# Attention probabilities of a gated attention + FFN block: one pass over the logits, with the turn done by DMA transposition

## The chip, the core and the metric

The kernel runs on one core of one Trainium2 chip, in one launch. The metric is the device time in microseconds; the time before is 1783.49 us, the median of 3 runs (1783.17 to 1783.70). Engines are named as in the profile: PE (TensorE matmul) and PEld (its weight loads), DVE (VectorE), ACT (ScalarE), POOL (GpSimd) and SP (SyncE, whose queue issues every DMA of this kernel; the profile calls its issuing "SPq").

## The reference, cut to what matters

Two branches read the same x (2048 tokens, 576 features) and are mixed by a gate per token. Branch A is attention with 32 heads of 18 features over 4 segments of 512 tokens, causal within a segment, plus a linear memory of the earlier segments; branch B is a SwiGLU FFN with 4608 hidden features.

```python
for s in range(N):                       # 4 segments of L = 512 tokens
    logits = einsum("bhqd,bhkd->bhqk", qs, ks) * scale + mask      # mask: -1e9 above the diagonal
    p = softmax(logits, axis=-1)
    a_dot = einsum("bhqk,bhkd->bhqd", p, vs)
    a_mem = (phi(qs) @ M) / (phi(qs) @ z + 1e-6)
    outs.append(g * a_mem + (1 - g) * a_dot)
    M, z = M + phi(ks).T @ vs, z + phi(ks).sum(...)
a = concat(outs) @ wo
b = (silu(x @ w_gate) * (x @ w_up)) @ w_down
return gate * a + (1 - gate) * b
```

## The kernel before, in words

Everything is computed to about fp32 accuracy out of sums of rounded terms: an fp32 operand is split into a high part (fp32r, bf16 or fp16) and a rest, and several matmuls are summed in PSUM.

**Stages.** First come the projections q, k, v of all segments and the memory branch (up to about 330 us of the span). q and k go to DRAM (`stk`) as three bf16 terms each. Then the FFN runs in two halves of 1024 tokens. A half has 36 positions, one for each tile of 128 hidden features (the loop at L1043). In a position PE makes seven products for gate and up (`seven`, L1035 and L1038). After every third position 16 groups of the down product (`down_groups`, L874) fall due, and they are worked off in the next position. In half 0 the split weights are also written to DRAM (`wc`, L257); half 1 reads them back (L682). A last stage turns the attention output, multiplies it by wo and mixes (L1160 on).

**Attention beside the FFN.** Attention is a generator, `att_gen` (L807). The hand-written function `beat` (L975) advances it by one step, tau, at chosen points of the FFN's program. In half 0 a step is taken only while down groups are due, so 10 steps stand in every third position and none in the other two; in half 1 the other positions take 4 or 5 steps each as well. The order on each engine is thus fixed by the program's text. One unit u is 2 heads of one segment (64 units, 8 matmuls of each kind a unit), and 5 steps work on the 5 PSUM banks of one unit:

- `s_bank` (L699): logits of query tiles i against keys 0..i, with the queries on the partitions. DVE adds the mask and takes the maximum of each row (L713, the masked logits themselves go to a scratch tile), into `mbs`. At the unit's last bank five small DVE instructions split the maxima into three bf16 terms and turn them in 32x32 blocks (L719 to L728).
- `m_store` (L730) writes those terms to DRAM (4 DMAs a unit) and `row_load` (L192) reads them back as 3 additional rows of `qst` (1 DMA). The `kst` tiles hold -1 in these rows.
- `t_bank` (L747), TL = 12 steps later: the same logits once more, now with the keys on the partitions and 111 rows, so that the maximum is subtracted by the matmul itself (L753). ACT takes Exp out of PSUM (L757), POOL zeroes what lies above the diagonal (L765).
- PL = 2 steps later DVE makes the fp16 high term of the probabilities (L843) and POOL the rest (L845).
- `pv_step` (L769): both terms are the stationary operands, v moves (L782, L784): 40 matmuls a unit. DVE sums the terms of v (L789), `o_step` (L795) divides, and the result goes to DRAM at a later step (`sends`, L812, or L849 at the end).

`stack_loads` (L175, issued at L819) brings in q and k of the next unit: 10 DMAs a unit, into one of NST = 4 buffers. `s_bank`, `t_bank` and `pv_step` share PSUM banks 5, 6 and 7 in turn (`ts_tile`).

All DMAs stand in SP's one queue in program order. In the built program each also waits for the DMA eight before it in that queue (8 semaphores in turn), so at most 8 are under way.

Of the kernel before, what the change touches and what calls it, by code (L numbers as in the profile page):

```python
# [12 lines left out]
F32 = mybir.dt.float32  # L13
# [7 lines left out]
P = 128  # L21
# [4 lines left out]
L = 512  # L26
# [11 lines left out]
NST = 4  # L38
TL = 12
PL = 2  # L40
VL = 3
# [22 lines left out]
def gated_mix(ctx, tc, xT, xrest, wf, wfr, wfh, wd, wv, wo, beta, cmask, ident, bmask, out):  # L64
# [11 lines left out]
    mxd = dram.tile([2 * NB, 3, 8, P], BF, name="mxd")  # L76
# [35 lines left out]
    ts_tile = banks(5, 6, 7)  # L112
# [60 lines left out]
    VP, accs, cur, unit, ms, mts, mbs = {}, {}, {}, {}, {}, {}, []  # L173
# [17 lines left out]

    def row_load(u):  # L192
        nc.sync.dma_start(qst[u % NST][KR:KR + 3].rearrange("z j (i n) -> z (j i) n", n=P), mxd[u])
# [76 lines left out]
    with ExitStack() as st:  # L270
# [293 lines left out]
        for s in range(NSEG):  # L564
# [41 lines left out]
            if s == 3:  # L606
# [4 lines left out]
                for i in range(NST):  # L611
                    if i < 2:
                        qst.append(kq.tile([P, 2, L], BF, name=f"qst{i}"))
                    if i < 2:
                        kst.append(kq.tile([P, 2, L], BF, name=f"kst{i}"))
                for i in range(2):
                    mbs.append(kq.tile([P, 8], F32, name=f"mb{i}"))
# [7 lines left out]
            for n in range(8):  # L625
# [10 lines left out]
                else:  # L636
                    if n == 4:
                        wraw_of[1] = [w_load(1, u) for u in range(2)]
                    if n < 2:
                        first_sum(6, n)  # L640
                    elif n < 6:
                        if n < 4:
                            nc.gpsimd.memset(f32(rhs[n - 2][96:]), 0.0)
                        if n == 3:
                            r_fetch(0)
                        if n - 2 < len(kst):
                            nc.gpsimd.memset(kst[n - 2], -1.0)
# [13 lines left out]
    with ExitStack() as st:  # L661
# [24 lines left out]
        kp = pool(ast, "kp", 2, side="right")  # L686
        ap = pool(ast, "ap", 2, side="right")
        for i in range(2, NST):
            kst.append(kp.tile([P, 2, L], BF, name=f"kst{i}", bufs=1))
        for i in range(2, NST):  # L690
            qst.append(kp.tile([P, 2, L], BF, name=f"qst{i}", bufs=1))
        for i in range(2, NST):
            defer(5 + i, lambda i=i: nc.gpsimd.memset(kst[i], -1.0))
        mqs = [kp.tile([P, 32], BF, name=f"mq{i}", bufs=1) for i in range(2)]
        for i in range(2):
            defer(9 + i, lambda i=i: nc.gpsimd.memset(mqs[i], 0.0))
        SPLAN = [[(0, 0, 3)], [(0, 1, 3)], [(384, 0, 0), (0, 0, 2)], [(384, 1, 0), (0, 1, 2)], [(0, 0, 1), (256, 1, 1)]]

        def s_bank(u, n):  # L699
            qs, ks = qst[u % NST], kst[u % NST]  # L700
            m = mbs[u % 2]
            bank = SPLAN[n]
            t = ts_tile()
            for c, pr, i in bank:
                w = P * (i + 1)
                nc.tensor.matmul(t[:, c:c + w], qs[:KR, pr, P * i:P * i + P], ks[:KR, pr, 0:w],  # L706
                                 start=True, stop=True)
                yield
            for c, pr, i in bank:
# [3 lines left out]
                nc.vector.tensor_tensor_reduce(scr[:, :w], t[:, c:c + w], cm[:, L - w:L], 1.0, -3.0e38,  # L713
                                               OP.add, OP.max, m[:, k:k + 1])
            if n == 4:
                mq = mqs[u % 2][:, :24].rearrange("p (z q) -> p z q", q=8)
                mr = kp.tile([P, 8], F32, name="mr")
                c = -SHIFT / SCALE
                nc.vector.tensor_scalar_add(mq[:, 0], m, c)  # L719
                nc.vector.scalar_tensor_tensor(mr, m, c, mq[:, 0], op0=OP.add, op1=OP.subtract)  # L720
                nc.vector.tensor_copy(mq[:, 1], mr)
                nc.vector.tensor_sub(mq[:, 2], mr, mq[:, 1])
                m_tr(u)
            yield

        def m_tr(u):
            mt = mts[u] = kp.tile([P, 32], BF, name="mt", bufs=1)
            nc.vector.transpose(mt, mqs[u % 2])  # L728

        def m_store(u):  # L730
            mt = mts.pop(u)
            d = mxd[u].rearrange("z q n -> (z q) n")
            for b in range(4):
                nc.sync.dma_start(d[:, 32 * b:32 * b + 32], mt[32 * b:32 * b + 24])

        def blk(pr, j, i):
            if j == 0:
                return pr, P * i
            if j == 1:
                return 2 + pr, P * (i - 1)  # L740
            if j == 3:
                return 2 + pr, 384
            return 4, 256 * pr + P * (i - 2)

        TPLAN = [[(0, 0)], [(1, 0)], [(0, 1), (0, 3)], [(1, 3), (1, 1)], [(0, 2), (1, 2)]]

        def t_bank(u, k):  # L747
            qs, ks = qst[u % NST], kst[u % NST]
            t = ts_tile()
            for pr, j in TPLAN[k]:  # L750
                _, c = blk(pr, j, j)
                w = L - P * j
                nc.tensor.matmul(t[:, c:c + w], ks[:KR + 3, pr, P * j:P * j + P], qs[:KR + 3, pr, P * j:L],  # L753
                                 start=True, stop=True)
                yield
            pe = ap.tile([P, L], F32, name="pe", bufs=4)
            nc.scalar.activation(pe, t, AF.Exp, scale=SCALE)  # L757
            if k < 2:
                d = pe[:, 0:P]
                pat = [[1, P]]  # L760
            else:
                st_ = 384 if k < 4 else 256
                d = bass.AP(tensor=pe.tensor, offset=pe.offset, ap=[pe.ap[0], [st_, 2], [1, P]])
                pat = [[0, 2], [1, P]]
            nc.gpsimd.affine_select(d, d, pattern=pat, compare_op=OP.is_ge, fill=0.0, base=0, channel_multiplier=-1)  # L765
            cur[5 * u + k] = pe
            yield

        def pv_step(z):  # L769
            u, k = divmod(z, 5)  # L770
            g, hf = divmod(u, 2)
            s, b = divmod(u, 16)
            if k == 0:
                unit[u] = ts_tile([P, 2, 4, 3 * E])
            t = unit[u]
            p1, p2 = cur.pop(("p", z))
            todo = [(pr, i, j) for pr, j in TPLAN[k] for i in range(j, 4)]
            for n, (pr, i, j) in enumerate(todo):
                h = 2 * b + pr
                v = VP[4 * s + h // 8][:, j, h % 8].rearrange("p t e -> p (t e)")  # L780
                c = blk(pr, j, i)[1]
                nc.tensor.matmul(t[:, pr, i, :], p1[:, c:c + P], v, start=(k == 0 and n == 0), stop=False,  # L782
                                 skip_group_check=True)
                nc.tensor.matmul(t[:, pr, i, 0:2 * E], p2[:, c:c + P], v[:, 0:2 * E], start=False,  # L784
                                 stop=(k == 4 and n == len(todo) - 1), skip_group_check=True)
            if k == 4:
# [20 lines left out]
        def att_gen():  # L807
            N = 10 * NB
            for tau in range(N + TL + VL + 5):
# [10 lines left out]
                z = tau - TL - VL - 1  # L820
# [420 lines left out]
```

## Time and profile before

| | us |
|---|---|
| median of 3 runs | 1783.49 |
| span of the profiled execution (first to last instruction) | 1782.1 |
| PE busy, 12381 matmuls | 1770.7 (99%) |
| PEld busy | 1521.5 (85%) |
| DVE busy | 1281.8 (72%) |
| ACT busy | 939.6 (53%) |
| POOL busy | 831.9 (47%) |
| DMA queue of the kernel, share of 16 engines | 61.0% |

The profiled execution has no time of its own besides its span; the median of the runs lies 1.4 us above it, which is what lies around the span. Busy times are unions of what ran on an engine; matmuls are pipelined, so the mean duration in a row is longer than what a matmul adds to a chain. SP's issuing isn't in the table of busy times; it is seen in the timeline of SP and in the views of single lines. The granted clock of PE is 1.000 over the whole span.

### The profile page before, as it was taken

Reading aid. Unit: us, or ns where it says so; the run is one execution under the profiler, and the core shown is the slowest. Engines: PE = TensorE matmul, PEld = TensorE weight load, DVE = VectorE, ACT = ScalarE, POOL = GpSimd, SP = SyncE. Lnnn points to the kernel's source line nnn. Section 1 sums busy time; section 2 is a strip of 40 time slices with the busy share of each in tenths; the row PEclk is TensorE's granted clock in tenths of the full one; section 3 lists DMA queues with packets and bytes.
Section 4 is the critical chain, followed back from the end, with each engine's and each line's share of the span. In section 5 each row is a group of like instructions: output and inputs, shape, how many; then the busy total and the mean of one; then the engine's idle time right before and its main releaser. Section 6 shows DMA issues by size and latency. Waiting matters only on the chain.

```text
span 1782.1 us, 36452 instructions
## 1 busy us (share of the span) xinstructions
PE 1770.7 (99%) x12381; PEld 1521.5 (85%) x12381; DVE 1281.8 (72%) x3309; ACT 939.6 (53%) x1718; POOL 831.9 (47%) x1064
## 2 busy tenths in 40 slices
PE   9999999999999999999999999999999999999999
PEld 7899978888888888888887887887887887888899
DVE  6657666878877777777777777777777778775455
ACT  7766565455645564556456445445445445445411
POOL 4434731444554455445535555555555555454121
PEclk9999999999999999999999999999999999999999
DMA  8645497677657865776496447547546456545644
GB/s 298 212 176 184 153 344 225 189 249 264 217 176 238 265 201 174 243 249 215 137 339 207 153 136 215 150 130 215 155 138 210 141 151 195 160 126 188 204 141 140
DMA packets 249418, 352.02 MB, mean 198 GB/s; under 512 B 90320, under 2 KB 130640, under 8 KB 249232
## 3 DMA queue, kind: packets, MB, share of 16 engines
q1 hardware_dynamic: 249232, 349.69, 61.0%
q8 instruction: 98, 1.61, 0.4%
q14 instruction: 88, 0.72, 0.1%
HBM read 210.72 MB, written 138.87 MB: 196 GB/s over the span
## 4 chain that ended last, share of the span: by engine, by line
PE 94%; DVE 2%; DMA 2%; ACT 1%; issue 1%; SPq 0%; DVEq 0%; ACTq 0%
PE bank L1035 37%; PE bank L874 25%; PE bank L138 12%; PE bank L1038 6%; PE bank L753 4%; PE bank L706 4%; PE bank L782 2%; PE bank L784 1%; PE bank L423 1%; PE bank L377 1%; DMA rh<-rc 1%; DMA wo__23740<-wc 0%; PE bank L947 0%; PE bank L385 0%; DMA draw<-in_wd_dram 0%
## 5 line engine op out<-in xcount | busy, mean ns | idle before, releaser
L874 PE MATMUL bank<-dw,hh 128*128 128x320 f32 (+1 forms) x2304 | 485.8, 303 | 1.6 <-DVE ya L883 1.0
L845 POOL TENSOR_TENSOR p<-pe,p 128x512 f16<-128x512 f32 x320 | 381.1, 1191 | 176.3 <-DVE p L843 115.6
L874 PEld LDWEIGHTS bank<-dw,hh 128*128 128x128 f32 x2304 | 378.1, 189 | 19.2 <-DVE ya L883 2.4
L757 ACT ACTIVATE pe<-bank 128x512 f32<-128x512 f32 x320 | 190.4, 595 | 363.5 <-PE bank L753 333.4
L874 PE MATMUL bank<-dw,hl 128*128 128x320 f32 (+1 forms) x1152 | 340.4, 295 | 1.0 <-DVE hl L116 1.0
L765 POOL TENSOR_SCALAR_AFFINE_SELECT pe<-pe 128x256 f32<-128x256 f32 (+1 forms) x320 | 140.3, 438 | 274.1 <-ACT pe L757 270.7
L713 DVE CUSTOM_DVE_ANT_0 scr<-bank,cm 128x512 bf16<-128x512 f32 (+3 forms) x512 | 247.5, 483 | 20.3 <-PE bank L706 12.3
L883 DVE TENSOR_TENSOR ya<-bank,ya 128x320 f32<-128x320 f32 x352 | 157.1, 452 | 102.1 <-PE bank L874 100.2
L874 PEld LDWEIGHTS bank<-dw,hl 128*128 128x128 f32 x1152 | 217.6, 189 | 1.5 <-DVE hl L116 1.5
L1038 PE MATMUL bank<-xr,rh 128*128 128x512 f32 x504 | 196.3, 390 | 0.9 <-DMA rh<-rc 0.9
L753 PE MATMUL bank<-qst,kst 111*128 111x512 bf16 (+3 forms) x512 | 151.5, 305 | 0.0
L843 DVE CAST p<-pe 128x512 f16<-128x512 f32 x320 | 150.3, 470 | 0.0
L706 PE MATMUL bank<-kst,qst 108*128 108x512 bf16 (+3 forms) x512 | 126.1, 300 | 0.4 <-DVE mb L713 0.4
L247 POOL TENSOR_TENSOR ws<-raw 128x256 f32<-128x256 f32 x72 | 66.7, 926 | 110.2 <-DMA raw<-in_wf_dram 53.8
L973 DVE TENSOR_TENSOR hl<-row,hh 128x512 fp32r<-128x512 f32 x120 | 102.0, 850 | 22.1 <-ACT hh L972 21.7
L1038 PEld LDWEIGHTS bank<-xr,rh 128*128 128x128 f32 x504 | 94.6, 188 | 21.6 <-issue 1.3
L1103 ACT ACTIVATE row<-bank 128x512 f32<-128x512 f32 x72 | 43.1, 599 | 125.7 <-PE bank L1038 125.7
L1108 DVE TENSOR_TENSOR row<-bank,row 128x512 f32<-128x512 f32 x72 | 49.7, 691 | 79.9 <-ACT bank L1107 79.9
L1118 DVE TENSOR_TENSOR row<-bank,row 128x512 f32<-128x512 f32 x72 | 49.6, 689 | 60.4 <-PE bank L1038 58.7
L1107 ACT ACTIVATE bank<-bank 128x512 f32<-128x512 f32 x72 | 41.9, 582 | 96.6 <-PE bank L1038 96.6
L138 PE MATMUL bank<-xo,qhi 128*128 128x512 f32 x288 | 91.0, 396 | 0.4 <-DVE xo L116 0.4
L753 PEld LDWEIGHTS <-kst 111*128 111x128 bf16 x512 | 48.3, 97 | 43.3 <-issue 24.8
(1688 smaller groups left out, 3997.9 us busy)
## 6 DMA issues: line engine op xcount, KB each, us to landing
rh<-rc SPq DMA_DIRECT2D x72, 336.0 KB
dc<-dw SPq DMA_DIRECT2D x36, 576.0 KB
dw<-dc SPq DMA_DIRECT2D x36, 576.0 KB
raw<-in_wf_dram SPq DMA_DIRECT2D x72, 256.0 KB
stk<-q SPq DMA_DIRECT2D x32, 384.0 KB
draw<-in_wd_dram SPq DMA_DIRECT2D x36, 288.0 KB
rc<-rt SPq DMA_DIRECT2D x42, 224.0 KB
vd<-vps SPq DMA_DIRECT2D x8, 912.0 KB
```

What stands on the lines that cost most here:

```text
L138: nc.tensor.matmul(t, st[n], mv[n], start=(n == 0), stop=(n == 13))
L706: nc.tensor.matmul(t[:, c:c + w], qs[:KR, pr, P * i:P * i + P], ks[:KR, pr, 0:w], start=True, stop=True)
L713: nc.vector.tensor_tensor_reduce(scr[:, :w], t[:, c:c + w], cm[:, L - w:L], 1.0, -3.0e38, OP.add, OP.max, m[:, k:k + 1])
L753: nc.tensor.matmul(t[:, c:c + w], ks[:KR + 3, pr, P * j:P * j + P], qs[:KR + 3, pr, P * j:L], start=True, stop=True)
L757: nc.scalar.activation(pe, t, AF.Exp, scale=SCALE)
L765: nc.gpsimd.affine_select(d, d, pattern=pat, compare_op=OP.is_ge, fill=0.0, base=0, channel_multiplier=-1)
L843: nc.vector.tensor_copy(p1, pe)
L845: nc.gpsimd.tensor_sub(p2, pe, p1)
L874: nc.tensor.matmul(t, p, q[:, cs], start=(f == CH * c and n == 0), stop=(f == CH * c + CH - 1 and n == 2))
L883: nc.vector.tensor_add(ya[:, i, cs], t, ya[:, i, cs])
L1035: nc.tensor.matmul(t, w[:, p, z], x[z][:, q], start=first and n == 0, stop=False, skip_group_check=True)
L1038: nc.tensor.matmul(t, rem[:, RPOS[j]], XR[j], start=False, stop=True, skip_group_check=True)
```

## The change

The logits are computed once. `t_bank`, `m_store`, `row_load`, the five small DVE instructions and the 3 additional rows go. Instead:

- `s_bank` keeps the masked logits, times -SCALE, in an fp32 tile `lg`, with the minimum of each row beside it; POOL adds SHIFT to each of these (one instruction on 128x1 for each of the 8 pieces of a unit).
- `e_bank`, a step later: Exp in place, one ACT instruction for each piece (8 a unit instead of 5), with the row's value as bias. What lies above the diagonal becomes 0 by the mask, so POOL's select goes.
- `c_bank`, two steps after `s_bank`: the two fp16 terms, into one tile `pq` of a head (128 queries x 2 terms x 1280 keys of all query tiles; 2 buffers).
- `turn`: one DMA transposition on SP's queue for each head (128 in all), from `pq` to `pk` (128 keys x 20 blocks x 128 queries; 2 buffers). In the built program each such instruction has blocks of 16 rows by 128 columns, 160 for a head's 640 KB, and waits for POOL's last rest of that head and, from the second unit on, for PE's reading of the `pk` buffer.
- `pv_step` works by head, three steps after the head's `turn` in program order. The S banks have PSUM banks 5 and 6, the pv sums bank 7.
- The order of banks in a unit changes, `stack_loads` has 2 buffers instead of 4, and `att_gen` runs 334 steps instead of 340.

PE issues 512 matmuls (and their weight loads) fewer; the number of instructions in SP's queue that move data stays at 1804 rows.

```diff
-NST = 4
-TL = 12
-PL = 2
-VL = 3
+NST = 2
+EL = 1
+CL = 2
+DL = 3
+VL = 6
...
+    s_tile = banks(5, 6)
+    pv_tile = banks(7)
...
+        SPLAN = [[(0, 0, 3)], [(384, 0, 0), (0, 0, 2)], [(0, 0, 1), (256, 1, 1)], [(0, 1, 3)], [(384, 1, 0), (0, 1, 2)]]
+        COL = (896, 1024, 512, 0)
...
-                scr = kp.tile([P, L], BF, name="scr", bufs=1)
-                nc.vector.tensor_tensor_reduce(scr[:, :w], t[:, c:c + w], cm[:, L - w:L], 1.0, -3.0e38,
-                                               OP.add, OP.max, m[:, k:k + 1])
...
+                nc.vector.tensor_tensor_reduce(lg[:, c:c + w], t[:, c:c + w], cm[:, L - w:L], -SCALE, 3.0e38,
+                                               OP.add, OP.min, m[:, k:k + 1])
+                nc.gpsimd.tensor_scalar_add(b[:, k:k + 1], m[:, k:k + 1], SHIFT)
+
+        def e_bank(u, n):
+            lg, b = cur[5 * u + n], mbs[u % 2][1]
+            for c, pr, i in SPLAN[n]:
+                z = lg[:, c:c + P * (i + 1)]
+                k = pr * 4 + i
+                nc.scalar.activation(z, z, AF.Exp, bias=b[:, k:k + 1], scale=-1.0)
+
+        def c_bank(u, n):
+            lg = cur.pop(5 * u + n)
+            for pr in ((0,), (0,), (0, 1), (1,), (1,))[n]:
+                h = 2 * u + pr
+                if h not in heads:
+                    heads[h] = ap.tile([P, 2, 10 * P], F16, name="pq")
+                a, w, c = ((0, L, 0), (0, L, L), (256 * pr, 256, 2 * L), (0, L, 0), (0, L, L))[n]
+                z, (p1, p2) = lg[:, a:a + w], (heads[h][:, k, c:c + w] for k in range(2))
+                nc.vector.tensor_copy(p1, z)
+                nc.gpsimd.tensor_sub(p2, z, p1)
+
+        def turn(h):
+            t = ap.tile([P, 20, P], F16, name="pk")
+            nc.sync.dma_start_transpose(t, heads[h].rearrange("p z n -> p (z n)"))
+            heads[h] = t
...
-            for tau in range(N + TL + VL + 5):
+            for tau in range(N + VL + 8):
...
-                if n == 1 and 1 <= u <= 2 * NB:
-                    m_store(u - 1)
-                if n == 3 and 1 <= u <= 2 * NB:
-                    row_load(u - 1)
+                for k, h in ((2, 0), (4, 1)):
+                    z = tau - k - DL
+                    if z >= 0 and z % 5 == 0 and z < N:
+                        turn(2 * (z // 5) + h)
...
+                for k, h in ((2, 0), (4, 1)):
+                    z = tau - k - VL
+                    if z >= 0 and z % 5 == 0 and z < N:
+                        pv_step(2 * (z // 5) + h)
+                if u < 2 * NB:
+                    s_bank(u, n)
+                z = tau - EL
                 if 0 <= z < N:
-                    runs.append(t_bank(z // 5, z % 5))
...
+                    e_bank(z // 5, z % 5)
+                z = tau - CL
                 if 0 <= z < N:
...
+                    c_bank(z // 5, z % 5)
```

More of the change, by code (lines that the diff above doesn't have):

```diff
@@ L684, in w_fetch @@
             return [(j + 2 if f else FIRST[j], lambda j=j: one(j)) for j in range(7)]
-        kp = pool(ast, "kp", 2, side="right")
         ap = pool(ast, "ap", 2, side="right")
[L688 to L697, printed above, removed]
+        SPLAN = [[(0, 0, 3)], [(384, 0, 0), (0, 0, 2)], [(0, 0, 1), (256, 1, 1)], [(0, 1, 3)], [(384, 1, 0), (0, 1, 2)]]
+        COL = (896, 1024, 512, 0)
         def s_bank(u, n):
             qs, ks = qst[u % NST], kst[u % NST]
[L701 to L704, printed above, removed]
+            m, b = mbs[u % 2]
+            t = s_tile()
+            for c, pr, i in SPLAN[n]:
                 w = P * (i + 1)
@@ L715, in s_bank @@
[L715 to L767, printed above, removed]
@@ L777, in pv_step @@
[L777 to L782, printed above, removed]
+            pt = heads.pop(h)
+            z = 2 * b + pr
+            todo = [(i, j) for i in range(4) for j in range(i + 1)]
@@ L786, in pv_step @@
-            if k == 4:
+                nc.tensor.matmul(t[:, pr, i, 0:2 * E], pt[:, 10 + c], v[:, 0:2 * E], start=False,
+                                 stop=(pr == 1 and n == len(todo) - 1), skip_group_check=True)
+            if pr:
                 if hf == 0:
```

60 lines of the change are left out of this document (18 added, 42 removed).

## The prediction

> **What bounds the kernel now.** I read the page's head and its chain first, then the stages, then SP's queue.
>
> ```profile
> span 1782.1 us, 36452 instructions
> ...
> PE 1770.7 (99%) x12381; PEld 1521.5 (85%) x12381; DVE 1281.8 (72%) x3309; ACT 939.6 (53%) x1718; POOL 831.9 (47%) x1064
> ...
> q1 hardware_dynamic: 249232, 349.69, 61.0%
> ...
> PE 94%; DVE 2%; DMA 2%; ACT 1%; issue 1%; SPq 0%; DVEq 0%; ACTq 0%
> PE bank L1035 37%; PE bank L874 25%; PE bank L138 12%; PE bank L1038 6%; PE bank L753 4%; PE bank L706 4%; PE bank L782 2%; PE bank L784 1%; PE bank L423 1%; PE bank L377 1%; DMA rh<-rc 1%; DMA wo__23740<-wc 0%; PE bank L947 0%; PE bank L385 0%; DMA draw<-in_wd_dram 0%
> ```
>
> PE bounds it: 94% of the chain that ended last is matmuls, and the second logits (L753), which the change removes, are 4% of it. Next, how densely attention stands in the stages; the views of two stretches, restricted to one line, count its matmuls: L706 (8 a unit), then L1038 (7 a position).
>
> ```profile
> 330.00:920.00 590.00, 37.83 (x154) 15.23 (x154) 1.00 0.68 223
> 920.00:1600.00 680.00, 83.21 (x338) 33.48 (x338) 1.00 0.57 169
> ```
> ```profile
> 920.00:1600.00 680.00, 84.14 (x216) 40.55 (x216) 1.00 0.57 169
> ```
>
> In half 1 338/8 = 42.25 units pass in 680 us, 16.1 us a unit, with 216/7 = 30.9 positions. In half 0 154/8 = 19.25 units pass, 2 in each burst of 10 steps. SP comes next, since the change puts 128 transpositions on its queue. The single lines show what one issue costs there (min/median/max ns):
>
> ```profile
> L819 SPq DMA_DIRECT2D qst<-stk x315: 292/770/1232, 271.1 to 1578.2; - x158
> ...
> L819 SPq DMA_DIRECT2D kst<-stk x315: 274/487/1027, 272.0 to 1579.0; - x158
> ...
> L734 SPq DMA_DIRECT2D mxd<-mt x256: 289/356/1357, 280.7 to 1602.5; - x128
> ...
> L193 SPq DMA_DIRECT2D qst<-mxd x64: 235/295/563, 289.0 to 1607.9; - x64
> ...
> L812 SPq DMA_DIRECT2D atd<-ob x31: 371/391/467, 457.3 to 1635.2; - x31
> ...
> L197 SPq DMA_DIRECT2D v<-vd x16: 581/592/620, 232.6 to 1524.5; - x16
> ...
> L862 SPq DMA_DIRECT2D dw<-dc x36: 320/372/1502, 935.5 to 1681.3; - x36
> ...
> L237 SPq DMA_DIRECT2D rh<-rc x72: 308/407/1728, 210.6 to 1668.1; - x72
> ```
> ```profile
> 1013.66 0.44 SPq L682 DMA_DIRECT2D wo__13625<-wc  x1
> ```
>
> A unit costs SP 5 x 0.770 + 5 x 0.487 = 6.29 us for q and k, 4 x 0.356 + 0.295 = 1.72 for the maxima, 0.391/2 + 0.592/4 = 0.34 for output and v: 8.35. A position of half 1 costs 7 x 0.44 + 0.372 + 0.407 = 3.86 us for weights, per unit 3.86 x 30.9/42.25 = 2.8. So SP issues for 11.2 of 16.1 us already. In half 0 it is tighter. The chain and SP's timeline over one burst:
>
> ```profile
> 433.40 1.31 PE bank L874 x9
> ...
> 475.09 4.34 DMA draw<-in_wd_dram
> ...
> 493.67 1.31 PE bank L874 x9
> ```
> ```profile
> 435.92 0.73 SPq L257 DMA_DIRECT2D wc<-wo__5262  x1
> 439.29 1.25 SPq L230 DMA_DIRECT2D rc<-rt  x2
> 440.64 0.62 SPq L257 DMA_DIRECT2D wc<-wo__5277  x1
> ...
> 445.31 0.34 SPq L232 DMA_DIRECT2D rr<-in_wfh_dram  x1
> ...
> 475.09 0.45 SPq L209 DMA_DIRECT2D draw<-in_wd_dram  x1
> ```
>
> From one burst's start to the next is 60.3 us. PE then waits 4.34 us for a weight tile that SP gets to only at 475.09: the burst's queue is late already. Only two stretches of the burst show SP waiting, 436.65 to 439.29 and 441.26 to 445.31, 6.7 us together.
>
> **The change, part by part.**
>
> *PE.* 512 matmuls go, 4% of the chain: 0.04 x 1782.1 = 71 us if nothing takes their place, 71/64 = 1.1 us a unit. The pv matmuls stay, in number and shape. The third PSUM bank goes from the logits to pv alone; with 5 logit banks a unit instead of 10, two suffice.
>
> *DVE, ACT, POOL.*
>
> ```profile
> L757 ACT ACTIVATE pe<-bank 128x512 f32<-128x512 f32 x320 | 190.4, 595 | 363.5 <-PE bank L753 333.4
> ...
> L845 POOL TENSOR_TENSOR p<-pe,p 128x512 f16<-128x512 f32 x320 | 381.1, 1191 | 176.3 <-DVE p L843 115.6
> ...
> L765 POOL TENSOR_SCALAR_AFFINE_SELECT pe<-pe 128x256 f32<-128x256 f32 (+1 forms) x320 | 140.3, 438 | 274.1 <-ACT pe L757 270.7
> ...
> L800 POOL TENSOR_TENSOR rz<-rz,omg 128x16 f32<-128x16 f32 x32 | 7.9, 248 | 28.0 <-DVE rz L799 27.2 <-DMA qst<-stk 0.8
> ...
> L1028 ACT ACTIVATE bg<-idt 128x1 f32<-128x1 f32 x58 | 11.8, 203 | 0.6
> ```
>
> Exp: 8 instead of 5 a unit over the same 2560 columns adds about three fixed parts of 0.2 us (L1028's 203 ns for one column), 0.6 x 64 = 39 us on an engine 53% busy that waits for PE. POOL loses 140 us of select and gains 512 adds of 128x1, at most 248 ns each (the row of 128x16), 127 us: nothing. DVE loses five small instructions a unit; its masked logits go to fp32 instead of bf16, for which two rows bound the price:
>
> ```profile
> L883 DVE TENSOR_TENSOR ya<-bank,ya 128x320 f32<-128x320 f32 x176 | 85.6, 487 | 53.3 <-PE bank L874 51.9
> ...
> L713 DVE CUSTOM_DVE_ANT_0 scr<-bank,cm 128x384 bf16<-128x384 f32 x128 | 71.3, 557 | 4.4
> ```
>
> 487/320 = 1.52 ns a column to fp32 against 557/384 = 1.45 to bf16: from nothing to 5% of 512 x 0.557 us, 14 us on an engine 72% busy; I take nothing. All this costs nothing as long as PE or SP covers it.
>
> *SP's queue.* Per unit 1.72 us for the maxima go and 2X come, X being the issue time of one transposition, which the trace doesn't show. From below: `dc<-dw`, 576 KB in plain rows, whose row is
>
> ```profile
> L857 SPq DMA_DIRECT2D dc<-dw x36: 319/422/499, 241.8 to 905.4; - x36
> ```
>
> so 0.42 us. From above: each of the 160 blocks as an issue of its own, 160 x 0.295 (L193) = 47 us. Between them lies the row in which SP puts a transfer together from pieces: the 10 q and k loads of a unit have 432 runs in 6.29 us, 14.6 ns a run. By bytes (640 KB against 54 KB in 0.770 us) that is 9.1 us a head. By runs, with two for each block, one for its reading and one for its writing, it is 320 x 14.6 = 4.7 us. A transposition is made of blocks, as those loads are of runs, so I stand nearest to this row and take **X = 4.7 us**.
>
> [...] No run here shows the transposition.
>
> *Half 1.* SP needs 6.29 + 0.34 + 2.8 + 2 x 4.7 = 18.8 us a unit, PE 16.1 - 1.1 = 15.0. SP becomes the bound: (18.8 - 16.1) x 42.25 = +114 us.
>
> *Half 0.* A burst has 4 transpositions, +18.8 us, less 2 x 1.72 = 3.4 of maxima, less the 6.7 us in which SP waited: +8.7 us behind a queue that PE already waits for. 590/60.3 is about 10 bursts: +87 us. PE's saving there doesn't show.
>
> *The end.*
>
> ```profile
> SPq L849 <- POOL ob L803: 13.0, 1, 13.0
> ```
> ```profile
> 1668.07 6.83 DMA rh<-rc
> 1674.97 6.97 DMA wo__23740<-wc
> ```
>
> The last output DMA (first row, SP's waits) blocks the queue for 13.0 us, and PE then waits 13.8 us for weights (the chain). With the change the last `o_step` stands six steps ahead of it, so the block goes: -13 us.
>
> *Waits added.* `turn` waits for POOL's last rest, issued just one step before; queued behind it are the weights and q and k. `m_store` had waited for DVE in the same way, so I count one against the other. DVE's cast of the head after next waits for the `pq` buffer, three steps on, 3 x 16.1/5 = 9.7 us: more than X and a landing. PE's pv has three steps as well.
>
> Sum against the execution's own 1782.1: +114 + 87 - 13 = 1970; the median lies 1.4 above the span: **1971 us**.
>
> **The rivals.**
>
> *Cheap transposition (faster).* SP stays under PE as long as 9.4 + 2X < 15.0, X < 2.8 us, and in a burst as long as 4X < 3.4 + 6.7, X < 2.5. With X at the plain row's 0.42 us PE keeps the bound: 1782 - 71 - 13 = 1698, about 1700 us. For it: the bytes are few, 128 x 640 KB over 16 engines at the page's mean rate (349.69 MB in 61.0% of 16 x 1782 us, 20 GB/s an engine) take 2.1 us a head. Against it: a head isn't rows but 160 blocks. [...]
>
> *Dear transposition.* X by bytes, 9.1 us: half 1 (9.4 + 18.2 - 16.1) x 42.25 = +486, half 0 (36.4 - 10.1) x 10 = +263: 2518 us. The same would follow if the engines moved 2560 runs of 256 bytes a head at the page's mean 70 ns a packet: 2560 x 0.07/16 = 11.2 us a head, beside a share of 57% in half 1 (9.2 us a unit): 31.6 us a unit, and DVE would stand at the `pq` buffers.
>
> *Between.* X of 2.5 to 3.5: half 1 ends near parity, time from 1710 to 1860.
>
> That the change doesn't do what it says is not one: the built program has 1024 PE rows fewer.
>
> **How the numbers follow.** Forecast (X 3.5 to 6, that is +(9.4 + 7.0 - 16.1) x 42.25 = 13 and (14 - 10.1) x 10 = 39 at one end, 224 and 139 at the other, so 1820 to 2130): 0.45. Cheap: 0.30. Dear: 0.20. Between: 0.05, of which 0.02 faster, 0.02 within 0.2% (what a measurement of this kernel can tell from no change), 0.01 slower. So faster 0.32, same 0.02, slower 0.66. The range reaches from the cheap rival, a little below 1700, to just short of the dear one's 2518: 1690 to 2500; what lies outside has about 0.15.
>
> **What would show it.** In the changed profile SP's timeline shows X directly: near 4.7 us confirms the step, under 2.8 the cheap rival. If right, the chain leaves PE (94% now) for SP and DMA in half 1, PE's busy share falls from 99% to (1771 - 71)/1970 = 86%, and half 1 takes about 18.8 us a unit. If X is small and the time still rises, the wait for POOL ahead of `turn` or the two `pq` buffers were wrongly priced at nothing; if X is small but landings take over 9.7 us, the engines are the bound. The 13 us at the end should be gone in every case.

## The result and the profile after

| | before | after |
|---|---|---|
| median of 4 runs each, us | 1783.42 (1783.17 to 1783.70) | 1975.41 (1973.65 to 1976.36) |
| ratio, 95% interval | | 1.1073 [1.1057, 1.1088] |
| span of the profiled execution, us | 1782.1 | 1972.9 |

The kernel is 10.7% slower; 1971 us was forecast. The page of the kernel after, in the parts that were shown of before (head, busy times, the granted clock in 40 slices, the DMA queue, the chain):

```profile
span 1972.9 us, 35124 instructions
...
PE 1784.2 (90%) x11869; PEld 1527.5 (77%) x11869; DVE 1205.9 (61%) x3053; ACT 1010.7 (51%) x1907; POOL 835.8 (42%) x1314
...
PEclk9999999999999999999979989989899989989999
...
q1 hardware_dynamic: 571408, 432.79, 78.3%
...
PE 57%; DMA 19%; SPq 9%; DVE 6%; issue 4%; POOL 3%; ACT 2%; DVEq 0%; ACTq 0%; POOLq 0%
PE bank L980 24%; PE bank L819 14%; PE bank L139 10%; DMA pk<-pq 10%; SPq L773 6%; PE bank L983 4%; DMA kst<-stk 2%; PE bank L690 2%; POOL pq L716 2%; DMA draw<-in_wd_dram 2%; SPq L720 2%; PE bank L736 1%; DMA rc<-rt 1%; DMA rh<-rc 1%; DVE lg L696 1%
```

PE had 94% of the chain and has 57%; DMA and SP's queue hold 28%, the transposition alone (`pk<-pq`) 10%. The queue moves 322,176 packets more and 24% more bytes. PE runs 512 matmuls fewer and is busy 13.5 us longer: its clock was 1.000 over the whole span and is now 0.960 in the mean, below 0.9 in six slices of the second half. SP issues 1841 DMAs instead of 2033 (320 for the maxima go, 128 transpositions come), so their number falls by 192; it does not stay the same, as the section on the change has it.

To see in which stage the time went I count the seven products of a position (L1038 before, L983 after; 7 a position). From the start of position 3 to that of 36 is "half 0", to that of 69 "half 1" (33 positions each), the rest "the end". Beside it, the view of one stretch of half 1, restricted to the line of the logits' matmuls (8 a unit); columns as in the prediction, the last three being granted clock, DMA share and GB/s. Before, then after:

```profile
960.00:1600.00 640.00, 79.65 (x324) 32.04 (x324) 1.00 0.55 164
```
```profile
960.00:1600.00 640.00, 64.75 (x255) 17.59 (x255) 0.91 0.84 199
```

324/8 = 40.5 units in 640 us are 15.8 us a unit; 255/8 = 31.9 are 20.1. In the table, "engines" is the DMA share times the us of a unit: the time for which all 16 engines work on a unit and the weights beside it.

| kernel | us | half 0 | half 1 | end | half 1: us a unit | DMA share | engines, us a unit | clock |
|---|---|---|---|---|---|---|---|---|
| before | 1783.4 | 668.8 | 709.9 | 146.3 | 15.8 | 0.55 | 8.7 | 1.00 |
| after | 1975.4 | 704.4 | 869.3 | 143.2 | 20.1 | 0.84 | 16.9 | 0.91 |
| e1 plain move | 1804.9 | 663.1 | 739.3 | 143.6 | 16.6 | 0.73 | 12.1 | 0.97 |
| e2 q, k on ACT | 1896.5 | 664.0 | 830.4 | 143.5 | 18.8 | 0.86 | 16.1 | 0.93 |
| e3 turn on ACT | 2036.2 | 718.5 | 916.0 | 142.8 | 20.7 | 0.91 | 18.9 | 0.91 |
| e4 turn later | 1964.4 | 702.8 | 859.7 | 143.3 | 19.6 | 0.84 | 16.5 | 0.93 |
| e5 no turn | 1851.9 | 680.6 | 770.5 | 142.4 | 17.6 | 0.51 | 9.0 | 0.96 |
| e6 plain, fillers | 2156.8 | 767.4 | 988.4 | 143.3 | 24.5 | 0.59 | 14.5 | 0.89 |
| e7 half turned | 1775.5 | 661.2 | 712.7 | 142.7 | 16.0 | 0.81 | 13.0 | 0.99 |
| e8 half, more buffers | 1764.1 | 658.1 | 704.5 | 143.6 | 16.3 | 0.83 | 13.5 | 0.99 |
| e9 steps spread | 1967.7 | 828.6 | 734.9 | 143.4 | (another split) | 0.85 | | 0.96 |
| e10 k on ACT | 1862.9 | 664.3 | 797.0 | 142.7 | 18.1 | 0.94 | 17.0 | 0.95 |
| e11 q on POOL, k on ACT | 1917.9 | 714.6 | 801.8 | 143.0 | 18.4 | 0.91 | 16.7 | 0.95 |
| e12 plain, k on ACT | 1763.5 | 653.9 | 708.4 | 143.0 | 16.3 | 0.76 | 12.4 | 0.98 |

The times of the experiments are of one run, so without an interval; the kernel before, run beside them, took 1782.19 (e1 to e4), 1784.70 (e5 to e8), 1784.13 (e9 to e11) and 1784.10 us (e12). In e8 and e12 the last unit starts at 1585 us; with the view ended at 1580 their 16.3 us are 16.0.

Of the loss of 191 us half 1 has 159 and half 0 36. What SP's queue does there, first by the single line of the transposition (min/median/max ns) and then in its timeline:

```profile
L720 SPq DMA_TRANSPOSE pk<-pq x128: 2370/3518/8014, 280.4 to 1804.6; - x128
```
```profile
1199.97 2.61 SPq L720 DMA_TRANSPOSE pk<-pq  x1
1202.64 0.80 SPq L773 DMA_DIRECT2D qst<-stk  x1
...
1210.35 0.61 SPq L676 DMA_DIRECT2D wo__14511<-wc  x1
1211.09 4.46 SPq L720 DMA_TRANSPOSE pk<-pq  x1
...
1226.88 0.43 SPq L807 DMA_DIRECT2D dw<-dc  x1
1227.35 0.44 SPq L676 DMA_DIRECT2D wo__14771<-wc  x1
1227.89 4.76 SPq L720 DMA_TRANSPOSE pk<-pq  x1
1232.69 0.57 SPq L235 DMA_DIRECT2D rh<-rc  x1
1233.37 0.37 SPq L807 DMA_DIRECT2D dw<-dc  x1
1233.78 0.43 SPq L676 DMA_DIRECT2D wo__14829<-wc  x1
1234.31 0.38 SPq L676 DMA_DIRECT2D wo__14850<-wc  x1
1234.79 6.07 SPq L720 DMA_TRANSPOSE pk<-pq  x1
```

SP issues almost without a break, and the price of one transposition isn't fixed: 2.61 us behind light traffic, 6.07 behind 336 + 576 + 2 x 256 KB of weights (the page's list of DMA issues; a `wo` tile is 128 x 512 in fp32) queued just ahead, and the 832 KB that stand before the transposition before it. Over the whole run, the 14 transpositions with under 400 KB issued in the 6 us ahead of them (by the start of the issues, a transposition counted as 640 KB) take 2.6 us in the mean, the 9 with over 2000 KB 6.4 us. The timeline of SP summed over 960 to 1600 gives 588 us of issuing in 640 us, 284.9 of it for 64 transpositions: X is 4.45 us here and 2.93 in half 0 (122.9 us for 42). The chain of the same time holds the landings (start, us); PE stands idle for 2.87, 0.80 and 1.84 us until `pk` has landed, up to 1234.90, 1244.47 and 1259.72:

```profile
1211.09 6.54 DMA pk<-pq
...
1227.89 16.54 DMA pk<-pq x2
...
1251.10 8.57 DMA pk<-pq
```

Issue and landing of one transposition stand on the chain for 6.5 to 8.6 us, where the shortest three steps between 960 and 1600 take 6.3 us in the kernel before (from the starts of L706's matmuls; the mean is 9.5).

### The profile page after: what moved, and what is told of

Read it like the earlier page. It is cut to its first block, busy times and chain, and to the rows that moved or that the text cites. A ratio compares the mean times of both kernels' runs of the same rounds, so it can differ in the third digit from the quotient of the medians.

```text
span 1972.9 us, 35124 instructions
## 1 busy us (share of the span) xinstructions
PE 1784.2 (90%) x11869; PEld 1527.5 (77%) x11869; DVE 1205.9 (61%) x3053; ACT 1010.7 (51%) x1907; POOL 835.8 (42%) x1314
## 2 busy tenths in 40 slices
DMA packets 571588, 435.04 MB, mean 221 GB/s; under 512 B 412688, under 2 KB 453008, under 8 KB 571408
## 3 DMA queue, kind: packets, MB, share of 16 engines
q1 hardware_dynamic: 571408, 432.79, 78.3%
## 4 chain that ended last, share of the span: by engine, by line
PE 57%; DMA 19%; SPq 9%; DVE 6%; issue 4%; POOL 3%; ACT 2%; DVEq 0%; ACTq 0%; POOLq 0%
PE bank L980 24%; PE bank L819 14%; PE bank L139 10%; DMA pk<-pq 10%; SPq L773 6%; PE bank L983 4%; DMA kst<-stk 2%; PE bank L690 2%; POOL pq L716 2%; DMA draw<-in_wd_dram 2%; SPq L720 2%; PE bank L736 1%; DMA rc<-rt 1%; DMA rh<-rc 1%; DVE lg L696 1%
## 5 line engine op out<-in xcount | busy, mean ns | idle before, releaser
L716 POOL TENSOR_TENSOR pq<-lg,pq 128x512 f16<-128x512 f32 (+1 forms) x384 | 393.0, 1029 | 134.4 <-DVE pq L715 107.3
L705 ACT ACTIVATE lg<-lg,nb 128x512 f32<-128x512 f32 (+3 forms) x512 | 268.0, 555 | 234.4 <-POOL nb L698 232.8
L698 POOL TENSOR_SCALAR nb<-mb 128x1 f32<-128x1 f32 x512 | 130.7, 255 | 430.0 <-DVE mb L696 413.2
L696 DVE CUSTOM_DVE_ANT_0 lg<-bank,cm 128x512 f32<-128x512 f32 (+3 forms) x512 | 233.0, 482 | 86.8 <-PE bank L690 83.9
L715 DVE CAST pq<-lg 128x512 f16<-128x512 f32 (+1 forms) x384 | 153.6, 410 | 127.8 <-DMA pk<-pq 118.2
L983 PE MATMUL bank<-xr,rh 128*128 128x512 f32 x504 | 203.3, 403 | 21.4 <-DMA rh<-rc 21.4
L736 PE MATMUL bank<-v,pk 128*128 128x57 bf16 x1280 | 87.3, 190 | 62.9 <-DMA pk<-pq 62.9
L736 PEld LDWEIGHTS <-pk 128*128 128x128 f16 x1280 | 72.9, 97 | 88.0 <-DMA pk<-pq 78.3
L983 PEld LDWEIGHTS bank<-xr,rh 128*128 128x128 f32 x504 | 98.7, 196 | 47.1 <-DMA rh<-rc 24.9
L1052 ACT ACTIVATE bank<-bank 128x512 f32<-128x512 f32 x72 | 41.9, 582 | 134.4 <-PE bank L983 134.4
L1038 ACT ACTIVATE bank<-bank 128x512 f32<-128x512 f32 x72 | 41.8, 581 | 134.1 <-PE bank L983 128.4
L690 PEld LDWEIGHTS <-qst 108*128 108x128 bf16 x512 | 35.2, 100 | 90.4 <-issue 66.1
L1053 DVE TENSOR_TENSOR row<-bank,row 128x512 f32<-128x512 f32 x72 | 49.7, 691 | 82.2 <-ACT bank L1052 82.2
```

What stands on the lines that cost most here:

```text
L696: nc.vector.tensor_tensor_reduce(lg[:, c:c + w], t[:, c:c + w], cm[:, L - w:L], -SCALE, 3.0e38, OP.add, OP.min, m[:, k:k + 1])
L698: nc.gpsimd.tensor_scalar_add(b[:, k:k + 1], m[:, k:k + 1], SHIFT)
L705: nc.scalar.activation(z, z, AF.Exp, bias=b[:, k:k + 1], scale=-1.0)
L715: nc.vector.tensor_copy(p1, z)
L716: nc.gpsimd.tensor_sub(p2, z, p1)
L736: nc.tensor.matmul(t[:, pr, i, :], pt[:, c], v, start=(pr == 0 and n == 0), stop=False, skip_group_check=True)
```

## The experiments

In the expectations A is the theory that SP's issuing is the bound, as forecast. B: the wait for POOL at the head of SP's queue. C: what the 16 engines have to do for the transposition, so its landing. L: the loop of two `pq` and two `pk` buffers. Other letters are told where they stand.

**e1: the same bytes as a plain move.** The blocks aren't turned, so what PE multiplies isn't the transpose.

```diff
-            nc.sync.dma_start_transpose(t, heads[h].rearrange("p z n -> p (z n)"))
+            nc.sync.dma_start(t.rearrange("p a n -> p (a n)"), heads[h].rearrange("p z n -> p (z n)"))
```

> The transposition of a head is replaced by a plain move of the same 640 KB within SBUF, at the same place in SP's queue and with the same waits (the probabilities are then not turned, so pv multiplies the wrong way round). Theory A, SP's issuing time is the bound: an issue falls from about 3.9 us to about 0.4 us and the time to 1690 to 1730 us. Theory B, the queue stands because each turn waits at its head for POOL (400 us of such waits in the changed kernel): little changes, 1930 us or more. Theory C, the 16 engines' time for 2560 runs of 256 bytes a head is the bound: as A here, 1690 to 1730 us, since the runs become long.

1804.93 us. The line of the move, and the page's queue:

```profile
L720 SPq DMA_DIRECT2D pk<-pq x128: 470/537/1555, 281.6 to 1634.6; - x128
```
```profile
q1 hardware_dynamic: 258064, 432.79, 71.6%
```

170 of the 192 us belong to the transposition as such. With it gone half 0 is 6 us shorter than before, but half 1 is still 29 us longer, where PE's saving should have made it shorter: no theory's number, and a loss that the plain move leaves.

**e2: q and k issued by ACT.** SP keeps the transpositions and the weights.

```diff
-                        nc.sync.dma_start(*d)
+                        nc.scalar.dma_start(*d)
```

> The 10 loads of q and k of a unit are issued from ACT's queue instead of SP's; all else is as in the changed kernel. Theory A: SP is relieved of 6.3 us of 18 a unit, the issuing fits under PE, 1720 to 1790 us (ACT then has some 400 us more to issue, about 80% busy). Theory B: the turns still wait for POOL at the head of SP's queue, 1930 us or more. Theory C: the engines move the same runs, 1900 us or more.

1896.51 us, far above A's range and a little under C's. Half 0 comes back whole (664 against 704): there SP's queue was the cause. Half 1 gains only 39 of 159 us, though SP issues for 329 of 640 us. The waits of ACT say why part of it stays:

```profile
ACT lg L705 <- DMA qst<-stk: 210.3, 54, 8.1
...
ACT lg L705 <- DMA kst<-stk: 71.6, 19, 6.3
```

As built, each of the ten loads a unit in this one queue waits for the eighth before it, and Exp stands behind them on ACT: 281.9 us in these two rows. POOL's rest then comes late, and here SP does stand before the transposition: 213 of the 640 us.

**e3: the transposition issued by ACT.**

```diff
-            nc.sync.dma_start_transpose(t, heads[h].rearrange("p z n -> p (z n)"))
+            nc.scalar.dma_start_transpose(t, heads[h].rearrange("p z n -> p (z n)"))
```

> The 128 transpositions are issued from ACT's queue instead of SP's. Theory A: SP has 7.8 us a unit less to issue, 1730 to 1830 us, with ACT some 500 us fuller. Theory B: the wait for POOL now stands at the head of ACT's queue and holds Exp and the FFN's activations, 1930 us or slower. Theory C: no change, 1900 us or more.

2036.16 us, worse, as B and C have it. Alone in its queue the transposition costs as much:

```profile
L720 ACTq DMA_TRANSPOSE pk<-pq x128: 2185/3301/11015, 281.1 to 1846.7; - x128
```

So its issue time isn't made by what stands ahead of it in its own queue. On ACT this time (3.3 us in the median) stands between the Exps, which is the likely reason for the longer run; no view separates it.

**e4: a step later.** `DL = 4`, `VL = 7` instead of 3 and 6.

> Each turn is issued one step later (DL 4 instead of 3) and pv with it (VL 7 instead of 6), so POOL's rest of the head has a whole step more before SP comes to the turn. Theory B: the waits of SP for POOL (400 us) mostly go, 1900 us or less. Theory A: SP has the same to issue, 1950 to 2000 us. Theory C: the two pq buffers are held a step longer for a landing, the same or slower, 1960 to 2050 us.

1964.44 us, 0.6% less, in the ranges of A and of C. B falls: a step more for POOL gives back 11 us of 192. Between 960 and 1600 SP stands idle right before the 64 transpositions for 19.5 us in the kernel after and for 8.5 us here (from the end of the issue ahead to the start of the transposition). The wait goes round to DVE's buffer, 118.2 us in the kernel after (below) and here:

```profile
DVE pq L715 <- DMA pk<-pq: 266.8, 79, 8.6
```

**e5: no move at all.** `pv_step` reads `pq` itself, unturned, and `VL = 3`.

```diff
-            t = ap.tile([P, 20, P], F16, name="pk")
-            nc.sync.dma_start_transpose(t, heads[h].rearrange("p z n -> p (z n)"))
-            heads[h] = t
+            heads[h] = heads[h].rearrange("p z (a n) -> p (z a) n", n=P)
```

> No transposition and no move: pv reads the tile pq as it is, not turned, and three steps earlier than in the changed kernel (VL 3); what is left out is the turn. It shows what everything else of the change is worth. Theory L (a loop of cast, POOL's rest, turn at the head of SP's queue, landing, next cast into one of two pq buffers) for the 105 us by which the plain move missed 1700: 1680 to 1715 us, half 1 some 50 us below before. Rival N (the loss is in the new chain of minimum, bias and Exp, or in the two PSUM banks for logits): 1760 us or more.

1851.92 us, in the range of rival N (1760 or more) and far above L's; but e7 and e12, which keep N's chain and its two banks, end below the kernel before. The run tells less than it should have, because PE now stands right behind POOL's rest:

```profile
PEld L736 <- POOL pq L716: 95.0, 78, 4.2
PE bank L736 <- POOL pq L716: 86.6, 78, 4.1
```

What it does give is the queue's work without any move:

```profile
q1 hardware_dynamic: 239632, 348.89, 59.1%
```

Share times span is 0.591 x 1850.1 = 1093 us of all 16 engines; after has 0.783 x 1972.9 = 1545, e1 0.716 x 1803.2 = 1291. A transposition therefore costs the engines (1545 - 1093)/128 = 3.5 us, the plain move of the same 640 KB 1.5 us.

**e6: plain move, and SP kept busy.** To e1 come 8 small DMAs a head, 24 x 64 bytes each, to have SP's occupation without the engines' work.

```diff
+            for k in range(8):
+                nc.sync.dma_start(fill[h, k], idt[:24, 4 * k:4 * k + 16])
```

> The plain move in place of the transposition, and behind each 8 DMAs of 1.5 KB to DRAM that nobody waits for: SP is occupied for about 3 us longer a head, as by a transposition, but the head's landing isn't later and the engines move no more. Theory A (SP's issuing time is what costs): 1920 to 1990 us, near the changed kernel. Theory C (engines and landing): 1805 to 1860 us, near the plain move without filling.

2156.80 us, 182 more than the kernel after and outside both ranges, at a DMA share of 0.59 in half 1. A fuller queue on SP thus costs time while the engines have room, but the dose was off, and issuing isn't separated from waiting. At a median of 365 ns

```profile
L724 SPq DMA_DIRECT2D fill<-idt x1024: 289/365/2266, 280.6 to 1989.5; - x171
```

the fillers should have taken 2.9 us a head; they take 0.48 us each in the mean, 3.9 a head, and between 960 and 1600 SP stands idle for another 0.19 us before each: they are eight more places in a queue where, as built, each waits for the eighth before (in the trace of the kernel after, all 1833 DMAs of SP from the ninth on have the semaphore of the eighth before). So it isn't shown that issuing time alone makes this loss.

**e7: half the blocks.** Only the high term is turned (80 blocks, 320 KB); POOL still makes the rest, into a tile that nobody reads, and the second product takes the high term again, so that every product stays. The rest of the probabilities is left out of the result.

```diff
-            t = ap.tile([P, 20, P], F16, name="pk")
-            nc.sync.dma_start_transpose(t, heads[h].rearrange("p z n -> p (z n)"))
+            t = ap.tile([P, 10, P], F16, name="pk", bufs=2)
+            nc.sync.dma_start_transpose(t, heads[h])
```

> Only the high term is kept and turned, 80 blocks instead of 160 a head (the rest term is computed by POOL into a scratch tile, and pv reads the high term twice); pq and pk have 2 buffers each as in the changed kernel. Theory A: X halves to about 2 us, SP's 13.4 us a unit fits under PE's 15.0: 1700 to 1760 us. Theory L: the landing shortens, but the loop of two buffers stays: 1780 to 1850 us.

1775.48 us, under the kernel before (1784.70), but 15 us above A's range and 5 below L's:

```profile
L721 SPq DMA_TRANSPOSE pk<-pq x128: 1259/1708/3682, 280.2 to 1604.8; - x128
```

The price halves from end to end (1.26 against 2.37 us at the least, 1.71 against 3.52 in the median), so it goes with the number of blocks, or with the bytes turned, which halve too; and with half of it all 192 us are gone. The engines' part falls too: 0.753 x 1773.7 = 1336 us, by e5's account (1336 - 1093)/128 = 1.9 us a transposition instead of 3.5. So e7 doesn't separate SP from the engines. It also takes away the wait for POOL, whose rest the transposition no longer reads; e4 and e12, where that wait stays, speak against this as the reason.

**e8: half the blocks, more buffers.** e7 with 4 `pq`, 3 `pk` and `VL = 8`.

> As the half turn, with 4 buffers for pq, 3 for pk and pv two steps later (VL 8). Theory L: the loop is open, 1690 to 1740 us, well below the half turn with 2 buffers. Theory A: within 1% of it.

1764.10 us, within 1% of e7, as A said. The buffers (L) are worth 11 us of e7's 1775.

**e9: steps of attention spread.** `TICK = ((0.5, 1.0), (0.42, 1.0))`: steps at the burst-free positions of half 0 too.

> The changed kernel with its steps of attention spread otherwise: half of them at the burst-free positions of half 0 too (159 steps in half 0 instead of some 120, so about 8 units leave half 1). All work stays. A (SP's issuing is the bound where units stand densely): half 1 needs 34 units x 18.2 us = 627 us of SP and is PE's again (about 690 us for 33 positions instead of 869), half 0 grows from 704 to about 750: 1840 to 1890 us. B (each turn costs its wait for POOL or for its landing wherever it stands): the price of a head is conserved and moves with it, about 1960 to 1990.

1967.67 us. Half 0 grows by 124 us and half 1 shrinks by 134: the price of a head moves with it, as B said, and A's 1840 to 1890 is missed. A thinner stream of units doesn't help, since half 0 has no room either: the view of its stretch 259 to 1087 (all engines) gives a DMA share of 0.86.

```profile
259.00:1087.00 828.00, 711.70 (x4810) 605.85 (x4809) 566.95 (x1409) 463.78 (x889) 408.72 (x656) 0.94 0.86 238
```

**e10: the k loads on ACT, q on SP**, five a unit in each queue.

```diff
-                    for d in stack_loads(u + 1)[6 * (n - 2):4 * n - 2]:
-                        nc.sync.dma_start(*d)
+                    for y, d in enumerate(stack_loads(u + 1)[6 * (n - 2):4 * n - 2]):
+                        (nc.scalar if y % 2 else nc.sync).dma_start(*d)
```

> The changed kernel with every second of the ten q and k loads of a unit on ACT's queue, the others on SP's. A (SP's issuing, and in the run with all ten on ACT only ACT's own queue, where the ninth load waits for the first of the same unit): SP issues about 465 us in half 0 and 600 in half 1, ACT isn't held for a landing, half 0 is back at 664 and half 1 comes to 720 to 760: 1795 to 1830 us. B (the buffers' ring and the wait for POOL bind half 1 whoever issues the loads): half 1 stays at 830, 1890 to 1910 us.

1862.91 us, the best run with the whole transposition. Half 0 is back at 664, as A said. Half 1 falls by 72 us to 797, short of A's 720 to 760, and the time lies between A's range and B's. The stretch shows what it runs into:

```profile
960.00:1600.00 640.00, 70.52 (x283) 19.31 (x282) 0.95 0.94 218
```

The 16 engines are busy for 94%. A unit took them 0.84 x 20.1 = 16.9 us in the kernel after and 0.94 x 18.1 = 17.0 here: about the same work in less time, until they are nearly full. (It isn't a fixed amount: e2 has 16.1, e3 18.9.) The chain has the landings at up to 13 us for two:

```profile
1235.42 13.32 DMA pk<-pq x2
...
1253.68 9.87 DMA pk<-pq
...
1275.66 10.67 DMA pk<-pq
```

**e11: k on ACT, q on POOL.** As e10, with `nc.gpsimd` in the place of `nc.sync`.

> The changed kernel with every second of the ten q and k loads on ACT's queue and the others on POOL's, none on SP's. A: SP issues 390 and 430 us as with all ten on ACT, half 1 700 to 750 us, 1780 to 1825 us in all. B (ring and wait for POOL): half 1 stays at 830, 1890 to 1910. D (issuing on POOL costs POOL more than 0.7 us a load): the rests come later, the turns with them, and the time stands above the run with ACT and SP by 5 x 64 x the difference, up to 1950 us.

1917.91 us. Half 1 is e10's (802), although SP issues for only 363 of 640 us there instead of 549: SP's issuing isn't the bound any more. That the engines are isn't shown by it, since D acts in half 1 as well: SP stands idle for 221 us right before the transpositions, and in the median POOL's rest ends 0.03 us before one starts (3.8 us in the kernel after). Half 0 loses 50 us against e10, which is D too:

```profile
ACT lg L705 <- POOL nb L698: 475.1, 207, 9.2
POOL qst L773 <- issue: 150.2, 76, 6.5
```

POOL's loads (600 ns each) delay the row values `nb`, and with them Exp.

**e12: e10 with the plain move of e1.** Again unturned.

> The run with every second q and k load on ACT's queue (half 1 797 us, engines 94% busy from 960 to 1600 us), with each transposition replaced by a plain move of the same bytes on the same queue; the blocks aren't turned, so what the pv products multiply isn't the probabilities' transpose. C (with SP relieved, the 16 engines' work on the transpositions binds half 1): half 1 falls to 680 to 715 us, the engines' share to about 0.80, 1745 to 1785 us in all. B (the wait for POOL ahead of each turn and the two pq and pk buffers bind it, whatever the DMA costs): half 1 stays within 15 us of 797, about 1850 us. Between, at the 739 us that the plain move had with all loads on SP: SP's queue isn't what held that run, and some 75 us of the loss belong to the order itself, 1800 us.

1763.47 us, inside C's range:

```profile
960.00:1600.00 640.00, 76.71 (x315) 21.27 (x315) 0.98 0.76 244
```

Half 1 in the four cells: transposition 869 with all loads on SP and 797 with k on ACT, plain 739 and 708. Against e10 only the kind of move differs, and 89 us go. The plain move relieves SP (328 of 640 us of issuing instead of 549) and the engines (0.76 instead of 0.94) together; that it is the engines that hold e10's half 1 is inferred from their 94% and not separated by a run. The 31 us between e1 and e12 lie in SP's queue, although SP issues for only 443 of 640 us in e1: it stands idle for 85 us right before the moves, with the loads queued behind.

## Why the prediction was right, and where it was not

**What bounds it: right, but half of the story.** SP's queue did become a bound: e2 and e10 give half 0 back whole and e10 72 of 159 us in half 1 by taking loads off it. But right behind SP stand the 16 engines, with 16.9 of 20.1 us a unit. That bound was weighed at both ends (2.1 us a head in the cheap rival, 11.2 in the dear) and not in the forecast; measured is 3.5 us. With it a unit's engine work is 17 us, more than the 15.8 us in which a unit passed before. From that I infer, and didn't try, that no order of issuing makes the full transposition pay in half 1. The two bounds are probably not independent: of the 4.45 us for which SP issues a transposition in half 1, 2.37 is the least, and the rest grows with what was issued just ahead.

**X = 4.7 us: the size is right in half 1, by luck; the model isn't.** Measured are 4.45 us in half 1, 2.93 in half 0, 3.52 in the median. It isn't so many ns a run: the least is 2.37 us, 14.8 ns for each of 160 blocks (15.7 in e7), and the rest grows with what was issued just ahead (2.6 to 6.4 us, above).

**Half 1, +114: measured +159.** SP issues 588/31.9 = 18.4 us a unit (18.8 forecast), but a unit takes 20.1. The failed step is that SP would issue without a pause. For 640 - 588 = 52 us of the stretch, 1.6 us a unit, it doesn't; over some 42 units that is 69 us. The view of SP's waits, over the whole run, names POOL ahead of `turn`:

```profile
SPq L720 <- POOL pq L716: 202.4, 62, 6.1
SPq L720 <- POOL nb L698: 198.0, 54, 6.2
```

These 400 us, which the expectations of e1 and e4 take for waits, mostly aren't. Between 960 and 1600 the same view has 214 us in these two rows, and SP is idle for 52 us in all:

```profile
SPq L720 <- POOL nb L698: 128.7, 31, 6.2
SPq L720 <- POOL pq L716: 85.7, 23, 6.1
```

The row of `nb` names an instruction whose result the transposition doesn't read: the view ends a wait at POOL's last signal before the issue is over, and that falls into the 4.45 us of issuing. In the trace, POOL's rest of the head has ended 3.8 us in the median before SP comes to the transposition. SP stands idle for 19.5 us right before the 64 transpositions, for 15.5 before loads of q and k and for 14.2 before weights. So the wait for POOL, set against the removed one of `m_store` and taken as nothing, is worth at most 0.6 of the 1.6 us a unit; what makes the other pauses isn't settled.

**"Three steps: more than X and a landing": failed.** The three steps were reckoned at the mean of 9.7 us. The mean is right (9.5 in the kernel before), but the shortest three take 6.3 us, and issue with landing 6.5 to 8.6 on the chain:

```profile
DVE pq L715 <- DMA pk<-pq: 118.2, 49, 8.0
...
PEld L736 <- DMA pk<-pq: 78.3, 43, 7.2
...
PE bank L736 <- DMA pk<-pq: 62.9, 39, 6.8
```

**Half 0, +87: measured +36.** The term was mis-sized through X: by the same working, 4 x 2.93 - 10.1 = 1.6 us a burst, 16 in all. The 4.34 us on the chain before weren't a wait of PE: it stands idle for 0.41 us there, up to 480.68. Why 20 more were lost isn't settled; e2 shows only that SP's queue holds all of it.

**The end, -13: measured -3.** `L849` waits no longer, but another DMA at the same place does, for a `dw` buffer that PE has to release:

```profile
SPq L807 <- PE bank L819: 16.1, 1, 16.1
```
```profile
1859.47 4.86 DMA me<-med
...
1865.65 4.93 DMA wo__21850<-wc
```

On the chain the landings behind it hold 9.8 us instead of 13.8. PE's own idle time until `wo` has landed is 0.75 us here and 0.34 in the kernel before, so 13.8 us weren't there to be gained. "In every case" was wrong: I had looked at what released the block, not at what stood next in the queue.

**PE's 71 us: too large, and mostly not time.** PE is busy 52 us less than before in e12 (1718.5) and 55.5 in e8 (1715.2). In e12, where neither SP nor the engines are full, the kernel is 21 us shorter than before; the rest of the saving doesn't reach the span even there. In the kernel after PE's share is 90% and not 86%, because its clock fell to 0.960 (last section).

**DVE, ACT, POOL at nothing: right as busy time.** That their longer chain costs no waiting isn't shown: some 31 us of PE's saving are missing in e12. Exp, POOL's add and the masked logits in fp32 (busy, mean ns):

```profile
L705 ACT ACTIVATE lg<-lg,nb 128x512 f32<-128x512 f32 (+3 forms) x512 | 268.0, 555 | 234.4 <-POOL nb L698 232.8
L696 DVE CUSTOM_DVE_ANT_0 lg<-bank,cm 128x512 f32<-128x512 f32 (+3 forms) x512 | 233.0, 482 | 86.8 <-PE bank L690 83.9 <-POOL pq L716 0.6 <-POOL rr L221 0.5
L698 POOL TENSOR_SCALAR nb<-mb 128x1 f32<-128x1 f32 x512 | 130.7, 255 | 430.0 <-DVE mb L696 413.2
```

ACT's 268 us are more than the 190 + 39 reckoned, on an engine busy for 51% of the span; POOL's 131 stand for 127; DVE's mean of 482 ns is what it had with bf16, 483:

```profile
L713 DVE CUSTOM_DVE_ANT_0 scr<-bank,cm 128x512 bf16<-128x512 f32 (+3 forms) x512 | 247.5, 483 | 20.3 <-PE bank L706 12.3
```

**The sum.** 1970 against a span of 1972.9 is nearer than its parts, which is luck: half 1 was 45 us too small, half 0 51 too large, the gain at the end 10 too large.

**The cheap rival falls.** It had SP issue a transposition in a plain row's 0.42 us. Here, for 640 KB within SBUF, a transposition takes more than the plain move of e1: 3.5 us of the engines against 1.5, 3.52 us of issuing against 0.54, and 1975 us in all against 1805.

**A version that beats both.** e8 does (1764.10 against 1784.70, one run each), without the rest of the probabilities in its result. Whether dropping the second product too, in either kernel, would gain more wasn't tried.

## What to carry to other kernels

Price a DMA transposition on two accounts, the issuing queue (here 2.37 us at the least for 160 blocks, 1.26 for 80) and the 16 engines (3.5 and 1.9 us); where the engines' work on a unit comes above the unit's time, other queues helped only in part here, and fewer blocks helped wholly. Compare the shortest spacing of the steps, not the mean, with the latency it has to cover. Set a sum of waits against the idle time of the same stretch before believing it. When a blocked DMA at the end of a queue goes, look which DMA stands next.

## What the runs showed of the hardware

- The issue of a transposition has no fixed price: with all its blocks the same it takes 2.4 to 8.0 us on SP and 2.2 to 11.0 on ACT, and more with more bytes issued just ahead (2.6 us below 400 KB, 6.4 above 2000). That the engines hold it back is the likely reading; no run varies this alone.
- The packets are small: 322,176 more in the kernel after than before. Against e5 that is (571,408 - 239,632)/128 = 2592 packets a head; in 3.5 us of 16 engines, 21.6 ns for one.
- PE's granted clock was halved behind pauses. In the kernel after it is 0.50 in 29 stretches of 3.4, 6.8 or 10.2 us, 157 us together, and 1.00 elsewhere; in the 9 us ahead of each of them a pause of PE of 1.09 us or more begins (one of 4.38 us ends at 433.50; the clock is 1.00 from 425.0 to 431.3, 0.50 from 431.4 to 438.1 and 1.00 from 438.2 to 445.0). Not every pause did it: of the 42 over 1.5 us, 31 have such a stretch begin within 9 us. In the kernel before no pause of PE is over 1.5 us and the clock is 1.00 over the whole span. So the mean is 0.91 in the stretch of half 1 where landings make PE pause, 0.99 in e7, and over the whole run 0.960 against 0.996 in e8, which runs the same 11869 matmuls in 1715.2 us of PE instead of 1784.2. The single line of the last of the seven products (min/median/max ns), the kernel after, then before:

```profile
L983 PE MATMUL bank<-xr,rh x504: 387/389/796, 221.8 to 1881.7; 128*128 128x512 f32 x168
```
```profile
L1038 PE MATMUL bank<-xr,rh x504: 388/389/467, 221.5 to 1689.9; 128*128 128x512 f32 x168
```

Two of the 504 take twice the median (796 and 792 ns) and 29 more over 480 ns; before, the longest took 467 ns. Of these 31, 24 lie in stretches at 0.50, the two among them; the other 7 take 497 to 500 ns at 1.00. The lower clock fits PE's being busy longer with fewer matmuls.
